# Loading the first half of V in natural order, copying it into key order on VectorE, and gating the constants on the end of the Sinkhorn

## The chip, the cores and the metric

One NeuronCore of a Trainium2 chip. The metric is the device time of one execution in microseconds, the median of the runs. PE is the matmul engine, PEld its weight load, DVE is VectorE, ACT ScalarE, POOL GpSimd, SP the engine that only starts DMAs here; PEq, DVEq, SPq are the instruction queues of these. "L257" is a line of the kernel.

## The reference, cut to what matters

```python
def _attn_ref(q, k, v, sort_net):            # q, k, v: (4, 8, 768, 64), sort_net: (4, 8, 8, 8)
    P = sort_net
    for _ in range(5):                       # "Sinkhorn": five times exp, rows to 1, columns to 1
        P = P - np.max(P, axis=-1, keepdims=True)
        P = np.exp(P)
        P = P / (np.sum(P, axis=-1, keepdims=True) + 1e-09)
        P = P / (np.sum(P, axis=-2, keepdims=True) + 1e-09)
    k_sorted = np.einsum('bhij,bhjcd->bhicd', P, k_b)      # the 8 blocks of 96 keys, mixed
    v_sorted = np.einsum('bhij,bhjcd->bhicd', P, v_b)
    ...                                      # softmax attention inside each block
def _moe_ref(x, w_ch1, w_ch2):               # after it: two FFTs, layer norm, MLP
    ...
```

## The kernel before

V is kept as 16-bit floats in `vcx`, 128 (batch, head, block) rows on the partitions. Its first half (`load_v(0)`, batches 0 and 1) is loaded already permuted into the order in which the attention takes keys (g, c, r for key 6c + 3g + r). So each contiguous piece is 3 keys x 64 = 192 values, 384 bytes on the chip.

```python
    load_qk(0, 0)                                        # K and Q of the first four heads, from POOL
    ...
    vcx = const.tile([128, 128, D], F16, name="vcx")
    dtab = vcx[:, 96:112, :].rearrange(...)              # a constant table shares the tile
    vv = v.rearrange("b h (i c g r) d -> (b h i) c g (r d)", i=NB, g=2, r=3)
    def load_v(t):
        for g in range(2):
            start(nc.gpsimd.dma_start(
                vcx[:, 48 * g:48 * g + 48, :].rearrange("p (c r) d -> p c (r d)", r=3),
                vv[128 * t:128 * t + 128, :, g, :]))
    load_v(0)
    load_qk(0, 1)                                        # K and Q of heads 4 to 7
    ...                                                  # Sinkhorn on DVE and ACT; ph[] are its ten divisions
    gated(nc.sync.dma_start(eb4[96:97], cn["erow"]...), ph[5])   # constants: the first waits for ph[5],
    start(nc.sync.dma_start(vsf[96:97, ...], cn["vrow"].ap()))   # the others follow it on SP
    start(nc.sync.dma_start(tab, cn["tab"].ap()))
    start(nc.sync.dma_start(dtab, cn["dtab"].ap()))
    start(nc.sync.dma_start(cs, cn["cs"].ap()))
    lt2 = const.tile([97, 2, S], F16, name="lt2")
    start(nc.sync.dma_start(lt2, cn["lt"].ap()))                 # 97 partitions
    ...
    for c in range(4):                                           # w1, from POOL, gated on ph[9]
        w = nc.gpsimd.dma_start(w1sb[:, c, :], w1v[:, c, :])
        gated(w, ph[9]) if c == 0 else start(w)
```

PE then works in this order. The means of V need all of V; the mix needs V in key order.

```python
    for n in range(6): v_mean(psm, n)       # 128x512 matmuls on V's first half tile (g = 0)
    ...                                     # the Sinkhorn matrix spread out, bdk made from it
    k0 = {0: kq(0, 0)}                      # K mixed, Q transposed, two heads
    for n in range(6, 12): v_mean(psm, n)   # on g = 1
    k0[0] = sc(k0[0])                       # scores, exp
    bdv_make(); q_copy(0, 1); k0[1] = kq(0, 1); vb_make(0, psm); k0[1] = sc(k0[1])
    load_qk(1, 0)                           # K and Q of batch 1, in POOL's queue behind w1
    for n in range(16): v_mix(0, n)         # reads vcx[:, :, d]
    ...                                     # the rest: attention, FFT, layer norm, MLP of four batches
    W = (64, 8, 8)                          # how far PE, DVE, ACT may be reordered in that rest
```

The softmax here doesn't subtract the row's maximum and nothing guards it: scores larger than these inputs give would overflow.

## Time and profile before

| | before |
|---|---|
| time, median (4 runs) | 333.45 us (332.79 to 335.56) |
| profiled execution | 802.83 us, slow |

The profiled execution was 2.4 times as long as the others (802.83 / 333.45), and its matmuls are slow from the start. What does not hang on PE in it, the loads and the DVE and ACT work of the start, can be read; a later profile of the same kernel in 333.16 us (run before_again below) has V landing at nearly the same time. Its trace holds no record of the clock at all; the windows below print 1.00 where there is no record, and that is no measured full clock. The head of its page, and the chain that ended last:

```profile
span 800.9 us, 5937 instructions
...
PE 772.6 (96%) x2444; PEld 366.4 (46%) x2444; DVE 206.0 (26%) x450; ACT 127.7 (16%) x254; POOL 38.8 (5%) x73
...
PE 95%; DMA 3%; DVE 1%; POOL 0%; issue 0%; ACT 0%; POOLq 0%
```

The chain is PE except for one DMA. The view of waits up to 60 us names it (columns: who waited, for whom, total us, times, longest), and the timeline shows when (start, duration, in brackets the idle time of the engine before it and what ended that):

```profile
PE pm_167 L257 <- DMA vcx<-in_v_dram: 19.6, 2, 12.5
```

```profile
2.96 2.29 POOL L218 DMA_DIRECT2D vcx<-in_v_dram  x2
...
10.29 0.35 SPq L296 DMA_DIRECT2D tab<-k_tab  x1
...
11.64 0.29 SPq L302 DMA_DIRECT2D lt_152<-k_lt  x1
...
12.54 4.89 PE L257 MATMUL pm_167<-vcx,pack 128*128 128x512 f16 x6 [12.54 <-DMA vcx<-in_v_dram]
...
28.22 5.05 PE L257 MATMUL pm_167<-vcx,pack 128*128 128x512 f16 x6 [7.00 <-DMA vcx<-in_v_dram]
```

Both halves of V were issued by 5.25 us. One landed by 12.54, the other only by 28.22, and PE stood still for it. The windows say what the DMA engines did meanwhile (after the engines' busy times: granted PE clock, mean busy share of the 16 DMA engines, above 1 where the times of their packets overlap, and GB/s):

```profile
core 0: us, PE busy (x) PEld busy (x) DVE busy (x) ACT busy (x) POOL busy (x), PEclk, DMA share, GB/s
8.00:14.00 6.00, 1.46 (x3) 0.44 (x3) 4.57 (x20) 1.48 (x4) 2.28 (x8) 1.00 1.60 196
14.00:22.00 8.00, 6.43 (x31) 3.07 (x30) 2.65 (x5) 0.75 (x2) 1.70 (x4) 1.00 1.25 284
22.00:28.00 6.00, 0.00 (x0) 0.00 (x0) 0.00 (x0) 0.00 (x0) 0.00 (x0) 1.00 1.15 224
28.00:34.00 6.00, 5.78 (x20) 1.92 (x21) 0.00 (x0) 0.07 (x1) 0.00 (x0) 1.00 0.94 194
34.00:40.00 6.00, 6.00 (x21) 5.77 (x17) 0.71 (x2) 2.77 (x6) 0.00 (x0) 1.00 0.08 17
```

From 34 us on 0.08 of the engines, about one of the 16, was still at work.

### The profile page before, as it was taken

What the parts mean: (1) busy time and instruction counts of PE and PEld (TensorE: products, weight loads), DVE (VectorE), ACT (ScalarE), POOL (GpSimd) and SP (SyncE); (2) the same over time, 40 slices, a digit from 0 to 9 for tenths busy, and PEclk for the clock granted to TensorE, in tenths of its full rate; (3) what the DMA queues carried; (4) which work ended last, traced back from release to release, by engine and by line L of the source; (5) the groups of instructions that cost most, each with busy time, mean ns of one, the idle gap of its engine ahead of it and who ended that gap; (6) DMA issues with size and microseconds to landing.
All of it is one profiled execution on the core that took longest, in us unless ns stands there. A gap on an engine that the chain in (4) does not pass through costs nothing.

```text
span 800.9 us, 5937 instructions
## 1 busy us (share of the span) xinstructions
PE 772.6 (96%) x2444; PEld 366.4 (46%) x2444; DVE 206.0 (26%) x450; ACT 127.7 (16%) x254; POOL 38.8 (5%) x73
## 2 busy tenths in 40 slices
PE   3699989999999999999999999999999999999998
PEld 1488856466676533432444454323433332433332
DVE  5032452222323211212413222123201212221211
ACT  2132332322352200100242201001200100100000
POOL 5010200100000000000000000001000000000000
DMA  9760582100022000100010000000100100000001
GB/s 198 151 97 1 83 100 38 26 15 0 1 40 40 6 13 26 20 6 26 14 20 14 14 13 20 1 26 13 20 13 27 20 0 26 21 13 26 14 0 39
DMA packets 33971, 24.90 MB, mean 31 GB/s; under 512 B 19124, under 2 KB 29876, under 8 KB 33942
## 3 DMA queue, kind: packets, MB, share of 16 engines
q0 software_dynamic: 19392, 13.63, 11.7%
q1 hardware_dynamic: 14552, 10.89, 4.5%
q8 instruction: 19, 0.31, 0.2%
q14 instruction: 8, 0.07, 0.0%
HBM read 29.10 MB, written 6.29 MB: 44 GB/s over the span
## 4 chain that ended last, share of the span: by engine, by line
PE 95%; DMA 3%; DVE 1%; POOL 0%; issue 0%; ACT 0%; POOLq 0%
DMA vcx<-in_v_dram 3%; PE pm_1289 L257 1%; PE pm_4011 L790 1%; PE pm_3015 L790 1%; PE pm_4030 L790 1%; PE pm_3857 L790 1%; PE pm_3838 L790 1%; PE pm_3655 L790 1%; PE pm_3625 L790 1%; PE pm_3461 L790 1%; PE pm_3419 L790 1%; PE pm_3209 L790 1%; PE pm_3179 L790 1%; PE pm_2336 L790 1%; PE pm_2306 L790 1%; PE pm_2112 L790 1%
## 5 line engine op out<-in xcount | busy, mean ns | idle before, releaser
L773 PEld LDWEIGHTS <-w1sb 128*128 128x128 f16 x512 | 90.4, 179 | 133.2 <-issue 132.2
L432 PEld LDWEIGHTS <-eb_83 97*128 97x128 f16 x384 | 53.1, 188 | 9.4 <-issue 9.2
L483 PEld LDWEIGHTS <-vcx 128*128 128x128 f16 x128 | 32.1, 252 | 5.1 <-issue 3.4
L257 PE MATMUL pm_167<-vcx,pack 128*128 128x512 f16 x12 | 9.9, 1095 | 19.6 <-DMA vcx<-in_v_dram 19.6
L257 PEld LDWEIGHTS <-pack 128*128 128x128 f16 x24 | 4.9, 208 | 29.1 <-issue 25.8
L790 PEld LDWEIGHTS <-hr_3258 128*128 128x128 f16 x48 | 9.0, 188 | 19.3 <-issue 19.3
L790 PEld LDWEIGHTS <-hr_3051 128*128 128x128 f16 x48 | 8.7, 181 | 19.9 <-issue 19.9
L790 PEld LDWEIGHTS <-hr_2208 128*128 128x128 f16 x48 | 8.6, 178 | 20.0 <-issue 20.0
L790 PEld LDWEIGHTS <-hr_3527 128*128 128x128 f16 x48 | 8.4, 175 | 20.2 <-issue 20.2
L790 PEld LDWEIGHTS <-hr_3895 128*128 128x128 f16 x48 | 8.4, 174 | 20.0 <-issue 20.0
L790 PEld LDWEIGHTS <-hr_3731 128*128 128x128 f16 x48 | 8.2, 172 | 20.1 <-issue 20.1
L790 PEld LDWEIGHTS <-hr_1372 128*128 128x128 f16 x48 | 8.5, 179 | 19.0 <-issue 19.0
L485 PEld LDWEIGHTS <-vbn_1305 128*128 128x128 f16 x64 | 13.6, 212 | 2.1 <-issue 1.9
L485 PEld LDWEIGHTS <-vbn_297 128*128 128x128 f16 x64 | 13.9, 217 | 0.5
L790 PEld LDWEIGHTS <-hr_2420 128*128 128x128 f16 x48 | 7.0, 155 | 14.2 <-issue 13.4
L388 PEld LDWEIGHTS <-ksb_88 64*128 64x128 f16 x128 | 6.5, 126 | 12.5 <-issue 12.5
L388 PEld LDWEIGHTS <-ksb_90 64*128 64x128 f16 x128 | 6.7, 134 | 8.3 <-issue 7.3
L740 PEld LDWEIGHTS <-lt_152 97*128 97x128 f16 x24 | 6.7, 280 | 8.1 <-issue 8.1
L257 PE MATMUL pm_1289<-vcx,pack 128*128 128x512 f16 x12 | 10.4, 1082 | 0.0
L790 PE MATMUL pm_3491<-w2sb,hr_3258 128*128 128x512 f16 x16 | 10.4, 858 | 0.0
L790 PE MATMUL pm_3461<-w2sb,hr_3258 128*128 128x512 f16 x16 | 10.3, 839 | 0.0
L654 PEld LDWEIGHTS <-pmt 128*128 128x128 f16 x48 | 8.8, 191 | 3.3 <-issue 0.4
(1300 smaller groups left out, 1385.9 us busy)
## 6 DMA issues: line engine op xcount, KB each, us to landing
vcx<-in_v_dram POOLq DMA_DIRECT2D x4, 768.0 KB, 14.9
w1sb<-in_moe_w_ch_dram POOLq DMA_DIRECT2D x4, 512.0 KB, 29.5
w2sb<-in_moe_w_ch_dram POOLq DMA_DIRECT2D x4, 512.0 KB, 10.3
cs<-k_cs SPq DMA_DIRECT2D x1, 579.0 KB, 8.4
tab<-k_tab SPq DMA_DIRECT2D x1, 514.0 KB, 6.5
k_70<-in_k_dram POOLq DMA_DIRECT2D x1, 384.0 KB, 5.3
q_72<-in_q_dram POOLq DMA_DIRECT2D x1, 384.0 KB, 6.2
k_79<-in_k_dram POOLq DMA_DIRECT2D x1, 384.0 KB, 29.1
```

Source lines behind the costliest of these rows:

```text
L257: nc.tensor.matmul(psm.rearrange("p c d -> p (c d)"), idh, vcx[:, 8 * n:8 * n + 8, :].rearrange("p c d -> p (c d)"), start=(n == 0), stop= ...
L388: nc.tensor.matmul(pss[h2][:, j, :], ks[rows, 4 * g + j], qt[rows, :, cc])
L432: nc.tensor.matmul(po[:, 65 * T:65 * T + 96], e[:, S * g + 256 * tt + 128 * n: S * g + 256 * tt + 128 * n + 128], vsf[:, vi:vi + 96], star ...
L483: nc.tensor.matmul(ps[:, dd, :], vcx[:, :, d], bd, start=True, stop=False)
L485: nc.tensor.matmul(ps[:, dd, :], vbn[t][:, d:d + 1].broadcast_to([128, 128]), bd, start=False, stop=True)
L654: nc.tensor.matmul(ps[pr, n, :], (fo if ci < 2 else fq)[:, ci % 2, 3 * n + t, :] if ci >= 0 else ee[:, 3 * n + t, 128:129], tab[:, t, NK * ...
L740: nc.tensor.matmul(ps, lt[:, 128 * T:128 * T + 128], rb, start=False, stop=True, skip_group_check=True)
L773: nc.tensor.matmul(ps, w1sb[:, c, 128 * fc:128 * fc + 128], ut[:, c, :], start=(c == 0), stop=(c == 3))
L790: nc.tensor.matmul(ps, hr[:, fc, 128 * tt:128 * tt + 128], w2sb[:, fc, :], start=(fc == 0), stop=(fc == 15))
```

## The change

Its intent: V's first half comes in with long pieces (48 keys, 6144 bytes on the chip, 1 per partition and DMA for 16), into a tile of its own in natural order; the means are taken from that tile; four DVE copies bring it into key order before the mix; and the constants start only when the Sinkhorn is done. The ordering windows of DVE and ACT go from 8 to 12. The whole diff:

```diff
@@ loads
-    load_v(0)
+    vst = wt([128, BLK, D], F16, "hr", 2, "vst")
+    vnat = v.rearrange("b h (i c) d -> (b h i) c d", i=NB)
+    for g in range(2):
+        start(nc.gpsimd.dma_start(vst[:, 48 * g:48 * g + 48, :],
+                                  vnat[0:128, 48 * g:48 * g + 48, :]))
@@ helpers
-    def v_mean(psm, n):
+    def v_sort(n):
+        nc.vector.tensor_copy(
+            vcx[:, 0:BLK, :].rearrange("p (g c r) d -> p g c (r d)", g=2, r=3)[
+                :, :, 4 * n:4 * n + 4],
+            vst[:, 24 * n:24 * n + 24, :].rearrange(
+                "p (c g r) d -> p g c (r d)", g=2, r=3))
+        op("DVE", 0.6)
+
+    def v_mean(psm, n, src=vcx):
         nc.tensor.matmul(
             psm.rearrange("p c d -> p (c d)"), idh,
-            vcx[:, 8 * n:8 * n + 8, :].rearrange("p c d -> p (c d)"),
+            src[:, 8 * n:8 * n + 8, :].rearrange("p c d -> p (c d)"),
@@ constants
-        "o (n s) -> o n s", n=NE)), ph[5])
+        "o (n s) -> o n s", n=NE)), ph[9])
@@ start of PE's work
     for n in range(6):
-        v_mean(psm, n)
+        v_mean(psm, n, vst)
@@ second run of means
     for n in range(6, 12):
-        v_mean(psm, n)
+        v_mean(psm, n, vst)
+    for n in range(4):
+        v_sort(n)
@@ windows of the rest
-    W = (64, 8, 8)
+    W = (64, 12, 12)
```

## The prediction

> **What bounds the kernel now.** The profiled execution took 802.8 us against 333.85 us unprofiled; [...]I read order, DMA and VectorE times from it and no PE times. PE is busy 96% (busy table). The chain of waits that ended last is PE's work (95%) behind one DMA: `vcx<-in_v_dram`, from 4.10 to 28.2 us. The view of waits has PE waiting 12.5 us for V's first half and 7.0 us (21.2 to 28.2) for its second, and once 3.6 us afterwards. So V's second half bounds the start, PE the rest.
>
> **Why it lands late.** The windows show about 195 GB/s from 6 to 14 us; at that rate V's 2 x 768 KB would land near 16.5 us. But the constants (1.67 MB) are issued from 9.71 us and share the engines with V's 384-byte packets; theirs are long (4112 and 4632 bytes for `tab` and `cs`). The DMA records show `lt` as 97 packets of 3072 bytes, one after another over 16 us, with V's last packets trickling beside them. This fits the Trainium skill, "DMA: Bandwidth & Descriptors", sections on why a DMA increments its semaphore by 16 (97 partitions have no divisor up to 16: one engine) and on queues (engines take turns between rings, packet by packet). The trace agrees: after 34 us only 0.07 of the engines is busy.
>
> **What the change does.**
> - Gate at the Sinkhorn's end (13.2 us): constants start 3.5 us later, when V is nearly through. Estimate from the rate: V lands near 12.3 and 16.5 us, and the wait is gone. The next heads' K and Q may land before 34 and 38 us; they are used after the mix of V.
> - Long descriptors: little by themselves; 4096-byte packets of w1 and V's of 384 bytes both move about 200 GB/s. POOL's issue, 1.15 us per half, shrinks.
> - Four VectorE copies of 1536 f16: a 768-element copy takes 0.33 to 0.40 us, so about 0.55 each, 2.2 us in all (estimate). VectorE idles 12.6 us before the first score's shift, so they fit while PE does means and scores: at most 1 us on the critical path.
> - Ordering windows of 12 for 8 may reorder the main part: within 2 us either way.
>
> **Sum.** In the profile PE should save the 7.0 us. Unprofiled, PE's work between 12.5 and 21.2 us is shorter, ending near 18.5 us by my estimate, so the wait is about 9.5 us, all critical. Less 0.5 for the copies: about 325 us. 8 in 10: 320.5 to 330.5. Chances: faster by over 2% 0.70, within 2% 0.28, slower 0.02.
>
> **What would show each step.** PE's second wait on V under 1 us, its first still near 12 us; V landed by 17 us; the chain of waits entering through Sinkhorn or VectorE, not V's load; the second run of mean matmuls near 21 us in the profile; four copies near 0.55 us, no score waiting on VectorE; the mix of V 7 us earlier (38 instead of 45.3 us).
>
> **What would make it wrong.** Unprofiled V lands earlier than in the profile, leaving less to win; the copies take 1.6 us each and hold the scores; the later constants, above all `lt` on one engine, delay K, Q or w1 until PE waits for them; the main part gives the gain back in its own waits; reordering costs more than 2 us.

## The result, and the profile after

| | before | after |
|---|---|---|
| time, median (4 runs each) | 333.45 us | 323.44 us (323.15 to 324.04) |
| ratio, 95% interval | | 0.9692 (0.9645 to 0.9738) |
| profiled execution | 802.83 us, slow | 323.5 us, fast; span 321.6 us |

A ratio is the mean time of one kernel's fast runs over the mean of the other's of the same rounds, so it is not quite the ratio of the medians.

The lines that answer to those of before: head of the page and chain, waits of PE, timeline, windows.

```profile
span 321.6 us, 5938 instructions
...
PE 290.4 (90%) x2444; PEld 181.8 (57%) x2444; DVE 203.0 (63%) x454; ACT 122.6 (38%) x254; POOL 40.1 (12%) x73
...
PE 70%; DMA 9%; ACT 9%; DVE 6%; issue 3%; POOL 2%; POOLq 0%; ACTq 0%
PE pm L802 26%; PE pm L785 24%; DMA q<-in_q_dram 9%; PE pf L749 7%; PE pf L444 4%; ACT ex L408 2%; PE pf L666 2%; PE pf L752 2%; PE pf L400 2%; ACT eb L424 1%; PE pf L375 1%; PE pf L386 1%; ACT vsf L167 1%; ACT un L714 1%; DVE eb L234 1%
```

```profile
PE pm L269 <- DMA vst<-in_v_dram: 12.2, 1, 12.2
PE pf L444 <- DVE eb L421: 4.5, 1, 4.5
PE pf L666 <- DVE ee L641: 3.6, 1, 3.6
```

```profile
2.95 1.09 POOL L226 DMA_DIRECT2D vst<-in_v_dram  x2
...
12.15 2.72 PE L269 MATMUL pm<-vst,pack 128*128 128x512 f16 x6 [12.15 <-DMA vst<-in_v_dram]
...
13.81 0.35 SPq L308 DMA_DIRECT2D tab<-k_tab  x1
...
15.15 0.29 SPq L314 DMA_DIRECT2D lt<-k_lt  x1
...
16.77 1.46 PE L269 MATMUL pm<-vst,pack 128*128 128x512 f16 x6
...
17.47 1.96 DVE L261 COPY vcx<-vst 128x1536 f16<-128x1536 f16 x4
...
18.61 1.97 PE L468 MATMUL pm<-pack,pdup 32*128 32x32 f32 x16
```

```profile
core 0: us, PE busy (x) PEld busy (x) DVE busy (x) ACT busy (x) POOL busy (x), PEclk, DMA share, GB/s
8.00:14.00 6.00, 1.85 (x5) 0.69 (x5) 4.57 (x20) 1.48 (x4) 1.19 (x2) 1.00 1.03 213
14.00:22.00 8.00, 6.76 (x85) 4.54 (x82) 6.33 (x16) 4.18 (x12) 2.37 (x5) 1.00 1.16 272
...
40.00:46.00 6.00, 4.99 (x92) 3.92 (x91) 5.54 (x16) 5.05 (x12) 2.78 (x4) 1.00 0.58 92
46.00:52.00 6.00, 1.51 (x30) 1.37 (x29) 2.04 (x5) 1.80 (x4) 2.17 (x3) 0.82 1.26 213
```

PE's second wait for V is gone: the second run of means follows the Q transposes at 16.77 us without a gap. But there is a new line: a DMA of Q takes 9% of the chain, and from 46 to 52 us PE worked 1.51 us of 6. The timeline there:

```profile
50.87 0.36 DVE L281 COPY qr<-q 128x768 f16<-128x768 f16 x1 [3.96 <-DMA q<-in_q_dram]
...
51.15 1.28 DVE L421 TENSOR_SCALAR eb<-ex 96x384 f16<-96x384 f32 x2
51.56 0.66 PE L444 MATMUL pf<-vsf,eb 97*128 97x96 f16 x6 [4.49 <-DVE eb L421]
```

DVE waited 3.96 us at the copy of batch 1's first Q. The shift of the exponentials (`eb`) that stands behind it in DVE's program, and ran after it, belongs to batch 0, and PE's attention matmuls waited 4.49 us for that. Of what the change won, part was given back here.

### The profile page after: what moved, and what is told of

It reads as the page before. It is cut to its first block, busy times and chain, and to the rows that moved or that the text cites. A ratio compares the mean times of both kernels' runs of the same rounds, so it can differ in the third digit from the quotient of the medians.

```text
span 321.6 us, 5938 instructions
## 1 busy us (share of the span) xinstructions
PE 290.4 (90%) x2444; PEld 181.8 (57%) x2444; DVE 203.0 (63%) x454; ACT 122.6 (38%) x254; POOL 40.1 (12%) x73
## 4 chain that ended last, share of the span: by engine, by line
PE 70%; DMA 9%; ACT 9%; DVE 6%; issue 3%; POOL 2%; POOLq 0%; ACTq 0%
PE pm L802 26%; PE pm L785 24%; DMA q<-in_q_dram 9%; PE pf L749 7%; PE pf L444 4%; ACT ex L408 2%; PE pf L666 2%; PE pf L752 2%; PE pf L400 2%; ACT eb L424 1%; PE pf L375 1%; PE pf L386 1%; ACT vsf L167 1%; ACT un L714 1%; DVE eb L234 1%
## 5 line engine op out<-in xcount | busy, mean ns | idle before, releaser
L785 PE MATMUL pm<-ut,w1sb 128*128 128x384 f16 x512 | 92.5, 327 | 0.0
L802 PE MATMUL pm<-w2sb,hr 128*128 128x512 f16 x384 | 86.8, 379 | 0.0
L785 PEld LDWEIGHTS <-w1sb 128*128 128x128 f16 x512 | 49.8, 100 | 32.9 <-issue 1.2
L802 PEld LDWEIGHTS <-hr 128*128 128x128 f16 x384 | 37.3, 99 | 42.7
L794 ACT ACTIVATE hr<-pm 128x384 f16<-128x384 f32 x47 | 22.9, 493 | 99.1 <-PE pm L785 99.0
L790 DVE TENSOR_SCALAR hr<-pm 128x384 f16<-128x384 f32 x81 | 44.8, 555 | 20.7 <-PE pm L785 17.1
L811 DVE TENSOR_TENSOR u<-pm,u 128x512 f32<-128x512 f32 x24 | 16.5, 687 | 40.9 <-PE pm L802 40.9
L408 ACT ACTIVATE ex<-pf 96x384 f32<-96x384 f32 x64 | 28.2, 489 | 11.8 <-PE pf L400 11.6
L444 PE MATMUL pf<-vsf,eb 97*128 97x96 f16 x384 | 21.3, 211 | 5.5 <-DVE eb L421 4.5
L714 ACT ACTIVATE un<-u,nm,ny 128x512 f16<-128x512 f32 x20 | 15.6, 809 | 25.3 <-POOL nm L702 19.5
L424 ACT ACTIVATE eb<-ex,negone 96x384 f16<-96x384 f32 x38 | 23.1, 622 | 0.3
L495 PE MATMUL pm<-bdv,vcx 128*128 128x128 f16 x128 | 21.9, 267 | 1.0 <-DMA vcx<-k_dtab 0.5
L756 DVE SCALAR_TENSOR_TENSOR u<-r,pf 128x512 f32<-128x512 f16 x24 | 16.3, 681 | 9.5 <-DMA out_dram<-u 5.7
L497 PE MATMUL pm<-bdv,vbn 128*128 128x128 f16 x128 | 21.6, 237 | 0.0
L495 PEld LDWEIGHTS <-vcx 128*128 128x128 f16 x128 | 20.1, 173 | 1.3 <-issue 0.9
L497 PEld LDWEIGHTS <-vbn 128*128 128x128 f16 x128 | 17.4, 136 | 0.7 <-issue 0.7
L759 DVE BATCH_NORM_STATS2 st<-u 128x6 f32<-128x512 f32 x24 | 16.5, 688 | 0.3
```

Source lines behind the costliest of these rows:

```text
L408: nc.scalar.activation(ex.rearrange("p j (c r) -> p j c r", r=6), pss[h2][0:96].rearrange("p j (r c) -> p j c r", c=16), AF.Exp, scale=SCALE)
L424: nc.scalar.activation(ed, src, AF.Identity, bias=negone[0:96])
L444: nc.tensor.matmul(po[:, 65 * T:65 * T + 96], e[:, S * g + 256 * tt + 128 * n: S * g + 256 * tt + 128 * n + 128], vsf[:, vi:vi + 96], star ...
L495: nc.tensor.matmul(ps[:, dd, :], vcx[:, :, d], bd, start=True, stop=False)
L497: nc.tensor.matmul(ps[:, dd, :], vbn[t][:, d:d + 1].broadcast_to([128, 128]), bd, start=False, stop=True)
L714: nc.scalar.activation(un, ul[tt], AF.Identity, scale=y[:, tt:tt + 1], bias=nm[:, tt:tt + 1])
```

## The experiments

Twelve kernels ran, and all gave the right result. In each table row the time is the median, the ratio is to the kernel before in the same rounds. The first four rows, the next four and the last four each ran as one set on one chip.

| run | what it is | time, us | ratio (95%) |
|---|---|---|---|
| before_again | before, for a profile | 333.16 (1 run) | |
| gate_only | before + gate | 323.54 | 0.9714 (0.968 to 0.9748) |
| long_only | after, gate back | 323.82 | 0.9719 (0.9684 to 0.9753) |
| after_w8 | after, windows back to 8 | 322.39 | 0.9679 (0.9642 to 0.9717) |
| before_lt96 | before, `lt` on 96 partitions | 328.1 | 0.9849 (0.9804 to 0.9893) |
| after_lt96 | after, `lt` on 96 partitions | 320.97 | 0.9643 (0.9605 to 0.9681) |
| after_qfirst | after, w1 behind batch 1's K and Q | 321.34 | 0.9664 (0.9622 to 0.9705) |
| w8_lt96 | after_lt96 with windows of 8 | 320.02 | 0.9617 (0.9575 to 0.9659) |
| after_again | after, as control | 324.11 | 0.9707 (0.9671 to 0.9743) |
| copies2 | after, each copy done twice | 323.95 | 0.9709 (0.9674 to 0.9744) |
| gate_lt96 | before + gate + `lt` on 96 | 321.55 | 0.9624 (0.9589 to 0.9659) |
| lt96_w8_12 | after_lt96, windows DVE 8, ACT 12 | 319.61 | 0.9577 (0.9542 to 0.9612) |

For the places in the program I read from each trace when the first matmul of a step started (us from the span's start; "attention 0 ends" is its last matmul's start):

```
                       before_again  after  after_lt96  w8_lt96  gate_only  long_only  before_lt96
second run of means           28.49  16.78       17.70    17.58      17.59      17.24        22.18
mix of V begins               38.59  23.95       25.93    25.49      24.46      25.47        32.28
attention 0 begins            52.17  38.41       40.73    39.50      38.63      40.25        46.81
attention 0 ends              61.29  53.98       51.52    48.62      47.75      54.01        55.92
first FFT matmul              67.45  59.12       56.97    54.76      57.98      59.15        62.07
last MLP begins              283.94 275.92      273.90   271.63     274.77     276.49       278.74
last matmul ends             327.49 317.89      315.88   315.22     318.32     318.45       322.33
```

### before_again: is the slow profile to be trusted for the start?

No edit.

> The kernel before, unchanged, for a profile in the fast state (the one at hand took 802.8 us). Theory A (the load of V was what was saved): PE's second wait for V is about 11.4 us, from 16.8 us (where the changed kernel begins its second run of mean matmuls) to 28.2 us, and neither PE nor VectorE waits over 1 us for a later q. Rival (unprofiled V lands earlier than in that slow profile, and the gain came from the reordering): the second wait is under 6 us.

```profile
PE pm L257 <- DMA vcx<-in_v_dram: 23.1, 2, 12.9
```

```profile
12.90 2.72 PE L257 MATMUL pm<-vcx,pack 128*128 128x512 f16 x6 [12.90 <-DMA vcx<-in_v_dram]
...
28.49 2.72 PE L257 MATMUL pm<-vcx,pack 128*128 128x512 f16 x6 [10.16 <-DMA vcx<-in_v_dram]
...
31.89 3.62 PE L456 MATMUL pm<-pack,pdup 32*128 32x32 f32 x16
```

V's two parts landed within 0.4 us of the slow profile. The wait was 10.16 us, since PE had reached it sooner, and no Q is waited for. Theory A holds; this is the profile to set against the one after. The state of one run is not known for certain, but its 333.16 us lies inside the runs of before on the same chip (331.95 to 335.12).

The milestones now give the account of the gain. The second run of means starts 11.7 us earlier (28.49 - 16.78), the mix of V 14.6 us earlier. The extra 2.9 us lie between the two: six mean matmuls took 2.72 us behind the wait and 1.46 us without it, sixteen f32 matmuls 3.62 us and 1.97 us. The wait did not slow them: the six before it had taken 2.72 us too, in both kernels. The records of the clock begin at 15.66 us in after, between its two runs of means, with the full clock, and only at 41.20 us in before_again. Then, by the end of attention 0, only 7.3 us are left of the 14.6.

### gate_only and long_only: which part does it?

```diff
-        "o (n s) -> o n s", n=NE)), ph[5])      # gate_only: the kernel before with this alone
+        "o (n s) -> o n s", n=NE)), ph[9])
```

> Only the gate of the constants moves (step 5 to the end of the Sinkhorn); V keeps its 384-byte packets, no copies, windows 8. Theory A (the gate does it): V landed by 18 us, PE's second wait for it under 2 us, time 322 to 326 us, and VectorE waits about 4 us for the first q of batch 1 (landing near 50 us), as in the changed kernel. Rival B (the long descriptors do it): V lands after 20 us and the time stays over 328 us.

```diff
-        "o (n s) -> o n s", n=NE)), ph[9])      # long_only: the kernel after with this alone
+        "o (n s) -> o n s", n=NE)), ph[5])
```

> The changed kernel with the gate put back to step 5. Theory A as the prediction had it (long descriptors do little by themselves): V lands after 22 us, time over 330 us. Rival B (long packets hold their own against the constants' packets, and V is nearly through when these begin at about 14.5 us): V lands by 18 us, time 320 to 325 us, and the wait for the first q of batch 1 is shorter than the changed kernel's 4.0 us, since lt starts 3.5 us earlier.

The times are 323.54 and 323.82 us, and either kernel alone lost the second wait for V. Waits of PE and of DVE in gate_only, then in long_only:

```profile
PE pm L257 <- DMA vcx<-in_v_dram: 13.0, 1, 13.0
...
DVE qr L269 <- DMA q<-in_q_dram: 4.2, 1, 4.2
```

```profile
PE pm L269 <- DMA vst<-in_v_dram: 12.0, 1, 12.0
...
DVE qr L281 <- DMA q<-in_q_dram: 2.2, 1, 2.2
```

So theory A holds for the gate and rival B holds for the descriptors: each is enough, and the two do not add up. My step "long descriptors: little by themselves" is refuted. The DMA records show why. The share of V's 1.57 MB whose packets had started:

```
                                   by 14 us   by 16   by 18   by 20   by 22   last packet starts
before_again  384 B, gate ph[5]        73%      78%     83%     99%     99%   27.9 us
long_only    6144 B, gate ph[5]        86%     100%                           15.9 us
gate_only     384 B, gate ph[9]        74%      98%    100%                   16.7 us
after        6144 B, gate ph[9]        87%     100%                           15.0 us
```

Times are from the span's start, as in the views; the expectations give some times of DMA packets (14.5, 22.0 and 28.6 us) on a scale that runs 0.5 to 0.7 us late. Two things are seen. Alone, between 10 and 14 us, short packets moved 48.4% of V in before_again (190 GB/s) and long ones 55.1% in after (217 GB/s): a gain of 14%. Beside the constants, which come at 14 us with packets of 2048 to 4632 bytes, the short ones moved 39 GB/s from 14 to 18 us (408 packets of V beside 348 of the constants, which moved 304 GB/s), while the long ones of long_only moved 143 GB/s from 14 to 15.5 us (35 packets beside 38). The Trainium skill, "DMA: Bandwidth & Descriptors", section "Queues, rings and completion order", says that each DMA engine takes turns between the queue rows it has work for, packet by packet, a packet there being typically 9 to 17 descriptors. The trace agrees as to the turns, by its own packets of one contiguous piece each: the two queues start about equally many, and so the queue of small packets moves a small part of the bytes. I had read that sentence before I predicted, and used it only to explain the lateness, not to ask what longer packets would do to the same contest.

The rival's other point holds in its number only: batch 1's Q was waited for 2.2 us and not 4.0, but it landed at 50.89 us, as in after (50.85); DVE came to it 1.8 us later.

### after_w8: the ordering windows

```diff
-    W = (64, 12, 12)
+    W = (64, 8, 8)
```

> The changed kernel with the ordering windows put back to 8. Theory A: 321.5 to 325.5 us, within 2 us of the changed kernel, since the windows do nothing for the start. Rival (the windows gave a good part of the 10 us): over 327 us.

322.39 us, ratio 0.9679 against 0.9692 and 0.9707 for the changed kernel in two sets: no difference that the intervals could show. In the profiles the windows move time about: from last MLP to last matmul it is 41.97 us in after and 43.58 us in after_w8, and attention 0 takes 9.12 us in w8_lt96 and 10.79 in after_lt96 (below), where only the windows differ.

### before_lt96: what held V until 28 us

`lt` has 97 rows, of which the kernel writes the last itself before it reads it. Loading 96 leaves the result as it was.

```diff
-    start(nc.sync.dma_start(lt2, cn["lt"].ap()))
+    start(nc.sync.dma_start(lt2[0:96], cn["lt"].ap()[0:96]))
```

> The kernel before, but lt is loaded without its last row (which the kernel writes itself before it reads it): 96 partitions for 97. Theory C (the last 1 % of V, from 22.0 to 28.6 us, waited only for lt on its one engine): V lands near 22 us, PE's second wait falls from 10.2 to about 4 us, and with no later wait for a q the time is 325 to 328 us. Rival (the other constants hold V until 28 us): unchanged, 331 to 334 us.

```profile
PE pm L257 <- DMA vcx<-in_v_dram: 16.8, 2, 12.7
```

The second wait fell from 10.2 to 4.1 us (16.8 - 12.7), as theory C had it, and the time to 328.1 us, 0.1 us outside what I expected. In the records the 97 packets of `lt` started one after another from 19.4 to 35.9 us; the 96 packets started from 18.4 to 20.1 us. The last 1% of V, which lasted from 20.5 to 27.9 us, was what stood beside `lt`: 46 packets of V started in that time and 45 of `lt`. This agrees with the Trainium skill, same page, section "Why a DMA increments its semaphore by 16 and not by 1": the number of engines is the largest one up to 16 that divides the outer sizes, and 97 leaves one engine. So of the 10.2 us of waiting, 6.1 were `lt` on its one engine; the other 4.1 stayed with `lt` spread out and went when all the constants came later (gate_only).

### after_lt96 and after_qfirst: what gave the gain back

after_lt96 is the same edit in the changed kernel. after_qfirst moves w1:

```diff
-    for c in range(4):                               # stood with the constants
-        w = nc.gpsimd.dma_start(w1sb[:, c, :], w1v[:, c, :])
-        gated(w, ph[9]) if c == 0 else start(w)
...                                                   # after load_qk(1, 0) and the mix:
+    for c in range(4):
+        start(nc.gpsimd.dma_start(w1sb[:, c, :], w1v[:, c, :]))
     for c in range(2):
         start(nc.gpsimd.dma_start(w2sb[:, 4 * c:4 * c + 4, :],
```

> The changed kernel with the same 96-partition load of lt. Theory C (14 us were gained by the first mix of V, and about 5 us given back because the first q of batch 1, queued behind w1, finishes at 50.85 us on the engine that lt keeps busy): q lands before 42 us, VectorE waits for it under 0.5 us, time 317 to 320 us. Rival (the 5 us are lost in the order of the main part, and q's wait only hides it): q lands early, time stays 322 to 324 us.

> The changed kernel, lt as it was, but w1's four loads issued after K and Q of batch 1 instead of before. Theory C: q lands by 42 us although lt still keeps one engine until about 50 us, wait for q gone, time 317 to 320 us; w1 lands by about 50 us, long before its first use at 85 us. Rival: time stays 322 to 324 us.

In after_lt96 the long wait for a Q is gone; batch 1's first Q took 14.2 us from issue to landing (24.67 to 38.82), in the changed kernel 28.8 us (22.08 to 50.85). There, from 40 to 44 us, 21 packets of K and Q (768 bytes each) started beside 21 of `lt`. The timeline answers to the one of after:

```profile
49.15 0.63 DVE L281 COPY qr<-q 128x768 f16<-128x768 f16 x1
49.70 1.26 DVE L421 TENSOR_SCALAR eb<-ex 96x384 f16<-96x384 f32 x2
50.10 0.69 PE L444 MATMUL pf<-vsf,eb 97*128 97x96 f16 x12 [0.71 <-DVE eb L421]
```

Attention 0 then took 10.8 us from its first to its last matmul, and 15.6 us in after (from the milestones), so 4.8 us are won back there. The time is 320.97 us, 1 us outside the 317 to 320 that I expected: this profile reached the mix of V 2.0 us later than after did, with its second means at the slower pace again. after_qfirst measured 321.34 us, also short of what I expected; that Q landed at 40.24 us and DVE's wait of 4.0 us for it is gone; a wait of 1.4 us for the next Q, at 60 us, took its place. Both edits act on the same wait by different means, and both remove it and lower the time; the mechanism is shown, its worth is some 1 to 3 us (by the ratios and by the medians) and not 4 to 6. The intervals of the ratios still overlap that of the changed kernel, so for the time alone these two runs are not proof.

### w8_lt96, gate_lt96 and lt96_w8_12: better versions

```diff
 # w8_lt96: after_lt96 and      W = (64, 8, 8)
 # gate_lt96: the kernel before with ph[9] for ph[5] and the 96 rows of lt, nothing else
 # lt96_w8_12: after_lt96 and   W = (64, 8, 12)
```

> The changed kernel with windows of 8 and lt on 96 partitions. With windows of 8 the wait for q was only 1.1 us, but PE still lost time near 53 to 59 us. Theory C: 317 to 320 us, as after_lt96. Rival (with windows of 8 little is lost to q, so that lt costs nothing there): 321.5 to 323 us.

> The kernel before with two lines changed only: constants gated at the end of the Sinkhorn, lt on 96 partitions; V's short packets, no copies, windows 8. If the gate and the wait for q are all there is: V lands by 18 us, no wait for q over 0.5 us, 319 to 321.5 us, as the w8_lt96 run (320.02). Rival (the long packets or the copies add something of their own): over 322 us.

> The changed kernel with lt on 96 partitions and windows of 8 for VectorE and 12 for ScalarE. The milestones show windows of 12 losing about 1.7 us up to the first attention's end and winning 1.6 us in the last MLP. If ScalarE's window makes the end and VectorE's the start, 318 to 319.5 us; if not, 320 to 321.5 us as the two run so far.

w8_lt96 measured 320.02 us: with windows of 8, where DVE waited for Q only 1.4 us in two waits (after_w8), the 96 rows still lowered the ratio from 0.9679 to 0.9617 (the two intervals just overlap). gate_lt96 reached 321.55 us, just over its range, in a set in which the kernel before took 333.56 us; its ratio 0.9624 is close to that of w8_lt96 (0.9617). Two changed lines, with V's short packets and without a copy, so do more than the whole change does (0.9707 in the same set, its interval wholly above).

These profiles also show what the wait for Q hangs on besides `lt`. Attention 0 takes 9.12 us in all seven profiles with a DVE window of 8, whether `lt` comes with 97 rows (before_again, gate_only, after_w8) or 96, and 10.8 to 16.3 us in the six with 12. With 8 the copy of that Q runs behind batch 0's shifts (in after_w8 the last shift at 47.74 us, the copy at 50.72), with 12 before some of them (in after the copy at 50.87, a shift at 51.15). With 8, then, the wait falls behind attention 0: its end and the first FFT matmul lie 10.2 us apart in gate_only and 6.1 in gate_lt96. So `lt` makes Q late, and the wider window lets attention 0 pay for it.

lt96_w8_12 is the fastest: 319.61 us where the control took 324.11 us. Its ratio's interval (0.9542 to 0.9612) lies below the control's (0.9671 to 0.9743), so this version beats both kernels. The time lies 0.1 us outside the range for my reason, and that reason was wrong: from last MLP to last matmul it takes 43.57 us, as with windows of 8 for both, so ACT's window doesn't shorten the end. Whether it differs from w8_lt96 at all stays open; the intervals overlap.

### after_again and copies2: what the copies cost

```diff
-    for n in range(4):
-        v_sort(n)
+    for n in range(8):
+        v_sort(n % 4)
```

> The changed kernel, unchanged, as the control of this set: 323 to 324 us, ratio 0.969 to 0.973, and again a wait of about 4 us of VectorE for the first q of batch 1.

> The changed kernel with every one of the four copies done twice (8 copies, 1.96 us more of VectorE, same result). If the copies are off the critical path, as predicted, the first mix of V starts at most 1 us later and the time is within 1 us of the control. Rival (the copies stand on the path, so that the change pays for them): about 2 us slower than the control, 325 to 326 us.

Eight copies (0.55 us each, from 17.4 to 21.3 us) gave 323.95 us where four gave 324.11 us in the same set. The first mix of V started at 24.18 us, against 23.43 in the control and 23.95 in the first profile. The copies are off the critical path, and so were four more. The control also repeated the wait for Q (4.7 us of DVE).

## Why the prediction was right

The time was 323.44 us for 325 predicted, inside the range, and faster by over 2%. Point by point:

- **The wait for V bounds the start: right.** It was 10.2 us at the usual pace of PE (before_again), predicted 9.5, and it went away. PE's second means start 11.7 us earlier: the wait, 0.75 us by V's first part landing earlier, and about 0.8 us of shorter matmuls before it.
- **V at 12.3 and 16.5 us: right.** PE began on the first part at 12.15 us, and the second part landed at 15.8 us.
- **The gate does it, long descriptors do little: half wrong.** The gate alone is enough (323.54 us), but so are the long descriptors alone (323.82 us). The step failed because I compared the two packet sizes only at times when V was alone (where they differ by 14%) and not in competition, where 6144-byte packets got 143 GB/s and 384-byte packets 39. The total did not show it, because the two are alternatives.
- **Four copies of 0.55 us, off the path: right.** 1.96 us for four; doubling them cost nothing. The Trainium skill, "VectorE: DVE Perf Modes", section "Side-by-side: where the cycles go for N=2048 bf16", makes such a copy of 1536 values (1536/4 + 8 + 150) / 0.96 GHz = 565 ns at four values a cycle (an estimate from that page); the trace has 551 to 555 ns.
- **A term missing: when the clock is released.** From second means to mix of V it took 10.1 us in both kernels that waited for V (before_again, before_lt96), and 6.7 to 8.4 us in the eleven profiles of kernels that did not: 1.7 to 3.4 us more gain. The first six means start about 0.43 us apart in all thirteen. The second six start 0.22 us apart in four (gate_only, after, after_again, copies2), where the first record of the clock, at its full rate, comes at 14.7 to 15.8 us. In the other seven without the wait that record comes at 19.7 to 21.3 us, and in the two with the wait at 37.7 and 41.2 us; there the second six start about 0.43 us apart again. This agrees with the Trainium skill, "TensorE: Matmul & The Clock Gate", Part 1, which has the array at half clock by default until a busy window of about 3.4 us, 426.7 against 215.7 ns for 512 columns. So the wait did not slow the array; it went with a later release. Why a kernel without the wait falls into one group or the other is not shown: after was twice in the early one, after_w8 and after_lt96 in the late one.
- **A term named as a risk and not counted: Q waits behind the constants.** The prediction said that the later constants, "above all `lt` on one engine", might delay K, Q or w1 until PE waits. It happened: 4.0 us of DVE, 4.5 of PE. after_lt96 and before_lt96 show `lt` as the cause on both sides of the change: first it held V, then Q (and attention 0 pays for Q only with a DVE window of 12). Where the gain went from mix of V (14.6 us) to the end of attention 0 (7.3 us): 0.9 us in the mix and before attention 0; of the 6.4 us in attention 0, rounded, 4.8 are `lt` and Q (15.6 against 10.8 us), 1.7 the order of the wider windows (10.8 against 9.1 us).
- **Windows within 2 us: right, in sum.** In these profiles they win 1.6 us in the last MLP and lose 1.7 us in attention 0 with 96 rows of `lt`; with 97 rows they lose 6.5 us there (15.6 us in after, 9.1 in after_w8) and get 2.0 us back by the first FFT matmul. The times still lie within 1.1 us (323.44 and 322.39 us), since after, in the early group of the clock, reached the mix of V 1.8 us sooner.

So the sum was right partly by luck: 11.7 + 2.9 - 7.3 + 0.7 (to the last MLP) + 1.6 (the last MLP) = 9.6 us. The prediction had 9.5 - 0.5 = 9.0 us; against that, 7.9 us of gain (2.7, 2.9, 0.7 and 1.6) and 7.3 us of loss were left out and nearly cancelled. The 9.6 us are the difference of the two spans (331.2 - 321.6).

## What to carry to other kernels

When a load that the critical path waits for shares the DMA engines with other queues, either start the others later or make its packets as long as theirs; one of the two can be enough, so try each alone before paying for both. Look for the one transfer with an awkward partition count (97 here) that keeps one engine busy long after the rest: here it delayed the end of the loads queued beside it, and when one victim was moved out of its way the next one showed. And when a start is moved forward by 14 us, list what lands at a fixed time and is needed soon after, because that is where the gain stops.

## What the Trainium skill lacked or had wrong

- "DMA: Bandwidth & Descriptors": it says that engines take turns between queues by packet, but not what that does to the shares. Here 384-byte packets fell to 39 GB/s beside packets of 2048 to 4632 bytes, and 6144-byte packets kept 143 GB/s mostly beside packets of 4112; alone they moved 190 and 217 GB/s (bytes as written).
- The same page gives 100 and 127 partitions as examples of few engines. A row count of 97 cost about 6 us of V's wait before the change and about 5 us of attention 0 after it (with windows of 12); leaving out one row was the cure (ratio 0.9849 for it alone; 0.9643 against 0.9692 in the changed kernel).
- "TensorE: Matmul & The Clock Gate" warns that trace events of the clock can be unreliable. In after they agree with the pace of the matmuls: the first, of the full clock, comes at 15.66 us, between means 0.43 and means 0.22 us apart. What misleads is the stretch before the first record: in before_again it begins at 41.20 us, and the windows print 1.00 before it, where 512-column matmuls start 0.43 us apart.
- The same page puts the release at about 3.4 us of sustained work and calls it variable. Here it came 2.6 to 3.5 us after PE's first mean in four profiles and 7.2 to 8.8 us after it in the seven others without the wait for V.
- The same page tells of a clock gate stuck at a quarter for over 50 us. The first profile of before took 802.83 us for 333.45, with 512-column matmuls of the means 0.84 us apart (0.43 in before_again), 384-column matmuls of the MLP 0.43 us apart (0.16), no record of the clock, and DMA, VectorE and ScalarE at their usual pace. No run here shows whether it is the same thing; its cause stays open.
